# Outputs of experts 0 to 6 turned by VectorE in squares of 32 and scattered as quarter rows

## The chip, the cores and the metric

The kernel runs on one core of one Trainium2 chip. The metric is the time of one execution on the device in microseconds (us); the median of three runs stands for the kernel. A profile is one further execution, recorded by the hardware profiler. Its span goes from the first to the last instruction.

The engines named below are TensorE (PE in the profile; PEld are its loads of the stationary operand), VectorE (DVE), ScalarE (ACT), GpSimd (POOL) and SyncE (SP), which only issues transfers. All data of this kernel are 32-bit floats.

## The reference

Attention with a threshold comes first, and its output is the input of a layer of experts to which tokens are assigned by a hash:

```python
batch, n_heads, seq, head_dim = (8, 8, 576, 64)        # attention
N, D, E, F = (4608, 512, 8, 1024)                      # experts

scores = scale * np.matmul(q, k.transpose(0, 1, 3, 2))
thresh = np.max(scores, axis=-1, keepdims=True) - tau
scores = np.where(scores >= thresh, scores, -1000000000.0)
attn = softmax(scores); x = attn @ v                   # x: (B*S, H*D)

expert_idx = token_ids * np.int64(2654435761) % np.int64(E)
for e in range(E):
    mask = expert_idx == e
    h = np.maximum(x[mask] @ w1[e], 0.0)
    out[mask] = h @ w2[e]
```

So 4608 tokens of 512 numbers each go through one of 8 experts, some 576 to each: two matrix products (512 to 1024, then 1024 to 512) with a ReLU between them. Each result row goes to its token's place in `out`.

## The kernel before, in words

**Stages.** Until about 480 us the kernel computes attention and writes x to a scratch tensor in memory (`x_scratch`); beside it, it sorts the tokens by expert (`route`, `scatters`). Then come the experts, one after the other. Only this second stage, and a few preparations at the end of the first (lines 812 to 820), are touched by the change.

**Tokens in slots.** Each expert has 608 slots, of which `caps` are used: 576 for the first five in the order of processing, 600 for the last three. Tokens without a slot go through a loop at the end. A slot is a pair (s, c): column 32 s + c of the expert's matrices, with s up to 18 and c up to 31. The table `stok` holds the token number of each slot; its 32 rows c stand four times, in each of the four groups of 32 partitions. `gidx`, copied from it, holds for 128 consecutive columns, one per partition, the token number to which the result goes.

**Features on partitions.** Both layers work on transposed data: x of an expert is `xT` (512 features as 4 blocks of 128 partitions, and a column for each slot), the hidden layer `h_0` has 8 such blocks, and the result is `oT` with 4. The stationary operand of a matmul is a block of a weight matrix (`w1_sb`, `w2_sb`), the moving operand 288 or 300 columns of `xT` or `h_0`.

**Seven products.** `seven` (line 908) computes a layer by Strassen's scheme in the form with seven products of half matrices. VectorE forms the sums of half matrices: `sums_w1`, `sums_w2` (four tensor_tensor instructions of 1024 elements a partition each, one of them in place in `w2_sb`), `sums_x` and `sums_h` (half as wide). In layer 1 the scheme runs twice (g = 0 and 1), with 8 matmul records for each product; in layer 2 once, with 16 for each. The order of the products is fixed: p1 (copied out of PSUM by ScalarE), c11, u2, u3, c21, one product that gives both u4 and c22, and c12. Six instructions of VectorE add a product from PSUM to a partial sum, and one product is read by two adds. A product lies in one of four PSUM tiles of two banks (`bank2`), which are used in turn; the document calls such a tile a bank.

**Order of the work.** The stage is written under a manual schedule: each engine takes its instructions in the order of the code. Side work is hung between the products by a callback with the number of the step (0 after c11, 1 after u2, 2 after u3, 3 after c21, 4 after c22, 5 after c12):

- in group 0 of layer 1 (`side1`) one sum of w2 at each step, and at step 0 the output of the expert before, `put_out(e - 1, (0, 1), (2, 3), (4,))`
- in group 1 of layer 1 the sums of the first half of h, and from step 3 of group 0 on the squares of the next x (`turns`)
- in layer 2 (`side2`) at step 0 what is left of the turns, then `fetch`, which has GpSimd gather the rows of x for the expert after the next (five indirect transfers), and from step 1 on the sums of the next w1 and x, two at a step.

The next x is turned without TensorE: VectorE transposes the gathered rows in squares of 32 (line 1025), and 16 transfers of SyncE move them into `xT` (line 1033).

**How an output leaves (before).** `put_out` turns `oT` back to rows. For each 128 columns TensorE does 8 transposes into a PSUM tile (line 989), 40 for an expert, in three PSUM tiles from the same ring of four. ScalarE copies each 128 rows to an output tile `o_sb`, of which there are three (line 1001), and GpSimd issues an indirect transfer that scatters 128 rows of 2 KB to their places in `out` (line 1005). The last expert's output leaves in smaller pieces during and after its own layer 2.

Of the kernel before, what the change touches and what calls it, by code (L numbers as in the profile page):

```python
# [9 lines left out]
FP32 = mybir.dt.float32  # L10
BF16 = mybir.dt.bfloat16
FP16 = mybir.dt.float16
I32 = mybir.dt.int32
# [7 lines left out]
def kernel(  # L21
# [81 lines left out]
    stok_odd = consts.tile([P, E, NB], I32, name="stok_odd")  # L103


    gidx = consts.tile([P, E, KT], I32, name="gidx")
    gidx_0 = consts.tile([P, KT, HP], I32, name="gidx_0")
    sidx = [consts.tile([P, KT], I32, name=f"sidx_{i}") for i in range(2)]
    gidx_x = consts.tile([P, E, KT], I32, name="gidx_x")
# [35 lines left out]
    with tc.tile_pool(name="a_q", bufs=1) as a_q, \  # L145
# [450 lines left out]
        def constants():  # L596

            nc.gpsimd.iota(iota_i[:], pattern=[[1, NOV]], base=0, channel_multiplier=0)
            nc.gpsimd.tensor_copy(iota_f[:], iota_i[:])
            make_upper_triangular(nc, u128[:], val=1.0, diag=False)  # L600
            nc.gpsimd.memset(ones128[:], 1.0)
            nc.gpsimd.memset(none[:], BIG)
            nc.gpsimd.memset(gidx[:], BIG)
            nc.gpsimd.memset(gidx_x[:], BIG)
            for t in sidx:
                nc.gpsimd.memset(t[:], BIG)
            nc.gpsimd.iota(tok[:], pattern=[[1, NTC]], base=0, channel_multiplier=NTC)
            for table in slot_dram:
                nc.sync.dma_start(out=table.rearrange("(p c) o -> p (c o)", p=P), in_=none[:])
# [83 lines left out]
        with tc.manual_schedule():  # L693
# [118 lines left out]
            nc.vector.tensor_tensor(out=stok[:], in0=stok[:], in1=stok_odd[:], op=ALU.min)  # L812
            for h in range(4):
                rows, n = slice(32 * h, 32 * h + 32), (NB - h + 3) // 4
                nc.vector.tensor_copy(gidx[rows, :, 0:n], stok[rows, :, h::4])
                nc.vector.tensor_copy(gidx[rows, E - 1, KT - 1:KT],
                                      stok[rows, E - 1, NB - 4 + h:NB - 3 + h])
            for g in range(4):
                rows, n = slice(32 * g, 32 * g + 32), min(KT, NB - KT * g)
                nc.vector.tensor_copy(gidx_x[rows, 1:, 0:n], stok[rows, 1:, KT * g:KT * g + n])  # L820
            for _ in pieces:
                pass
            for kt in range(KT):
                fetch_0(kt, HP - 1)
            fill(FO * 2 * (CO - 1) - 18)
# [3 lines left out]
    with tc.tile_pool(name="m_x", bufs=1) as m_x, \  # L829
         tc.tile_pool(name="m_o", bufs=3) as m_o, \  # L830
         tc.tile_pool(name="m_s", bufs=1) as m_s:

        F2, C2, FH, D2, NG = F // 2, CO // 2, FO // 2, DIN // 2, FO // 4
        xT_bufs = [xT_0, m_x.tile([P, CO, CAP], FP32, name="xT_1")]
        xq = m_x.tile([P, DIN // 32, 32 * KT], FP32, name="xq")
        oT = m_x.tile([P, CO, CAP], FP32, name="oT")
        o_end = m_x.tile([P, DIN], FP32, name="o_end")
        mark = m_x.tile([P, 1], FP32, name="mark")
        w1_s = m_s.tile([P, 3, C2, F2], FP32, name="w1_s")
# [27 lines left out]
        def w1_blocks(w):  # L867
            return [w[:, C2 * j:C2 * j + C2, F2 * i:F2 * i + F2] for i in range(2) for j in range(2)]

        def w2_blocks(w):  # L870
            return [w[:, FH * j:FH * j + FH, D2 * i:D2 * i + D2] for i in range(2) for j in range(2)]

        def x_blocks(e):
            x, half = xT_bufs[e % 2], caps[e] // 2
# [16 lines left out]
        def sums_w2(e):  # L891
            s1 = None
            if e == E - 1:
                spare = w_pool.tile([P, CO, F], FP32, name="w1_sb")
                s1 = w_tiles["s1"] = spare[:, :, 0:D2]
            return left(*w2_blocks(w_tiles[e, 2]), triple(w2_s, 0, FH), s1)

        def sums_x(e):
            return right(*x_blocks(e), triple(x_s, 0, C2, caps[e] // 2))
# [8 lines left out]
        def seven(a, a_s, b, b_s, m0, outs, relu, after):  # L908

            (a11, a12, s1, a22), (s2, s3, s4) = a, a_s  # L910
            (b11, t1, b21, b22), (t2, t3, t4) = b, b_s
            c11, c12, c21, c22 = outs
            n_k, width = a11.shape[1], b11.shape[2]
            p1, u2, u3, u4 = (t[:, :, 0:width] for t in halves)

            def product(x, y):
                ps = bank2()
                for i in range(2):
                    c0 = m0 + P * i
                    for c in range(n_k):  # L920
                        nc.tensor.matmul(ps[:, i, 0:width], lhsT=x[:, c, c0:c0 + P], rhs=y[:, c],  # L921
                                         start=c == 0, stop=c == n_k - 1)
                return ps[:, :, 0:width]

            def out(c, ps, u, step):
                add(c, ps, u)()
                if relu:
                    nc.scalar.activation(c, c, AF.Relu)  # L928
                after(step)

            nc.scalar.copy(p1, product(a11, b11))  # L931
            out(c11, product(a12, b21), p1, 0)
            add(u2, product(s2, t2), p1)()
            after(1)
            add(u3, product(s3, t3), u2)()
            after(2)
            out(c21, product(a22, t4), u3, 3)
            k5 = product(s1, t1)
            add(u4, k5, u2)()
            out(c22, k5, u3, 4)  # L940
            out(c12, product(s4, b22), u4, 5)
# [10 lines left out]
        def layer2(e, side):  # L952

            w, half = w_tiles[e, 2], half2(e)
            outs = [oT[:, C2 * i:C2 * i + C2, half * k:half * k + half]
                    for i in range(2) for k in range(2)]
            a = w2_blocks(w)
            if e == E - 1:
                a[2] = w_tiles["s1"]
            seven(a, triple(w2_s, 0, FH), h_blocks(0, FH, half),  # L960
                  triple(h_s, 0, FH, half), 0, outs, False, side)

        def last_tile(middle):

            w, o_sb, idx = w_tiles[E - 1, 2], o_end, gidx[:, E - 1, KT - 1:KT]
            rows = CAP - 2 * CHL
            for c0, c1 in ((0, DIN - P), (DIN - P, DIN)):
                ps = bank2()
                for fo in range(FO):
                    nc.tensor.matmul(ps[0:rows, 0, 0:c1 - c0], lhsT=h_0[:, fo, 2 * CHL:CAP],  # L970
                                     rhs=w[:, fo, c0:c1], start=fo == 0, stop=fo == FO - 1)
                    if (c0, fo) == (0, FH - 1):
                        middle()
                nc.scalar.copy(o_sb[0:rows, c0:c1], ps[0:rows, 0, 0:c1 - c0])
            put_rows(o_sb[0:rows], idx[0:rows])

        def put_out(e, *groups):

            def rows_of(kt):
                return t_rows(e, kt) if e < E - 1 or kt < KT - 2 else 2 * CHL - FIRST[kt]  # L980

            trs = [bank2() for _ in groups]
            for tr, kts in zip(trs, groups):
                for i, kt in enumerate(kts):
                    rows = rows_of(kt)
                    for co in range(CO):
                        for r in range(2):
                            half, c0 = slice(64 * r, 64 * r + 64), D2 * i + 64 * co
                            nc.tensor.transpose(tr[0:rows, r, c0:c0 + 64],
                                                oT[half, co, FIRST[kt]:FIRST[kt] + rows],  # L990
                                                ident[half, half])
            for tr, kts in zip(trs, groups):
                for i, kt in enumerate(kts):
                    rows = rows_of(kt)
                    o_sb = m_o.tile([P, DIN], FP32, name="o_sb")
                    dst = o_sb[0:rows].rearrange("p (c r q) -> p r c q", c=CO, r=2)
                    src = tr[0:rows, :, D2 * i:D2 * i + D2].rearrange("p r (c q) -> p r c q", c=CO)
                    if e == E - 1 and kt % 2:
                        nc.vector.tensor_copy(dst, src)
                    else:  # L1000
                        nc.scalar.copy(dst, src)  # L1001
                    put_rows(o_sb[0:rows], gidx[0:rows, e, kt:kt + 1])

        def put_rows(o_sb, idx, ordered=False):
            inst = nc.gpsimd.indirect_dma_start(  # L1005
                out=out[:, :], out_offset=bass.IndirectOffsetOnAxis(ap=idx, axis=0),
                in_=o_sb, in_offset=None, bounds_check=N - 1, oob_is_err=False)
            inst = getattr(inst, "ins", inst)
            if ordered:
                return  # L1010
            tc.declare_no_dep(inst, group="rows", reason="every token has one slot: distinct rows")
            tc.add_to_no_dep_group("rows", inst)
# [35 lines left out]
        with tc.manual_schedule():  # L1048
            for e in range(E):
# [3 lines left out]
                if e > 0:  # L1053
                    w2_work, h_work = sums_w2(e), sums_h(e, 0, 2)

                    def side1(g, step):
                        if g == 0:
                            run(w2_work)
                            if step == 0:
                                put_out(e - 1, (0, 1), (2, 3), (4,))  # L1060
                        else:
                            run(h_work)
                        if step > 2:
                            run(turns, 1 if g == 0 else 2)

                    layer1(e, side1)
                    run(sums_h(e, 2, FH), 4)
# [4 lines left out]
                def side2(step):  # L1072
# [3 lines left out]
                            fetch(e + 2)  # L1076
                    else:
                        run(x_work, 2)
                    if not more and step == 4:
                        put_out(e, (0,))  # L1080

# [84 lines left out]
```

## Time and profile before

| what | value |
|---|---|
| median of the runs | 944.61 us (943.98 to 944.72) |
| profiled execution, its own time | 938.01 us |
| its span | 936.4 us, clock of TensorE 0.997 |
| TensorE busy | 919.9 us (98%) |
| VectorE busy | 731.2 us (78%) |
| ScalarE busy | 476.4 us (51%) |
| GpSimd busy | 308.6 us (33%) |
| transposes of L989, TensorE | 312 in 11.5 us |
| evictions of L1001, ScalarE | 37 of 584 ns |
| scatters of L1005, GpSimd | 39 of 1192 ns |
| squares of L1025, VectorE | 35 of 691 ns |

The profiled execution is 6.6 us (0.7%) shorter than the median of the runs; the profile is used for durations and for where the time lies. The busy time of TensorE is a union of pipelined, modelled records, so the starts of its matmuls tell more than its busy share. In the table of groups a line says: source line, engine, operation, output and inputs, shapes and count, then busy time in us, the mean of one instruction in ns, the idle time of the engine just before them and what ended it. Line numbers are those of the kernel before; in the changed kernel they are up to 34 higher.

### The profile page before, as it was taken

How to read it: one execution, taken by the hardware profiler on the slowest of the kernel's cores; microseconds unless marked ns; L12 is line 12 of the kernel's file. 1: busy time of each engine (PE TensorE's matmuls, PEld its weight loads, DVE VectorE, ACT ScalarE, POOL GpSimd, SP SyncE). 2: the span in 40 equal slices, each digit the busy share in tenths (PEclk: the TensorE clock that was granted, in tenths of full speed). 3: DMA queues.
4: the chain of work that ended last, by engine and by line, in shares of the span. 5: the costliest groups of instructions: out<-in, count | busy, mean ns of one | idle time of the engine just before them, and what ended most of it. 6: DMA issues, size and time to landing. Idle time of an engine off the chain costs nothing.

```text
span 936.4 us, 21124 instructions
## 1 busy us (share of the span) xinstructions
PE 919.9 (98%) x7775; PEld 643.1 (69%) x7775; DVE 731.2 (78%) x1643; ACT 476.4 (51%) x776; POOL 308.6 (33%) x424
## 2 busy tenths in 40 slices
PE   8999999999999999999999999999999999999996
PEld 4666666666666666666577777777777777777785
DVE  8999999999999999999457665756667566675541
ACT  6888888888988988988511120202112031120310
POOL 4233332336676643556135210403013030100202
PEclk9999999999999999999999999999999999999998
DMA  7355464464456776751016545254443544311101
GB/s 176 92 144 128 105 145 116 111 150 113 93 128 190 180 167 161 199 135 47 18 25 206 168 98 186 83 158 156 103 180 99 154 153 141 137 51 29 53 1 53
DMA packets 113351, 113.12 MB, mean 121 GB/s; under 512 B 31018, under 2 KB 87866, under 8 KB 113248
## 3 DMA queue, kind: packets, MB, share of 16 engines
q1 hardware_dynamic: 105168, 92.64, 37.5%
q0 software_dynamic: 7648, 18.91, 6.9%
q8 instruction: 63, 1.03, 0.5%
q14 instruction: 40, 0.33, 0.1%
q10 hardware_dynamic: 432, 0.21, 0.1%
HBM read 81.99 MB, written 21.47 MB: 110 GB/s over the span
## 4 chain that ended last, share of the span: by engine, by line
PE 61%; issue 29%; DVE 3%; ACT 2%; POOL 2%; DMA 2%; POOLq 0%; SPq 0%; DVEq 0%; ACTq 0%
PE av L314 18%; PE sc L236 15%; PE bank L921 12%; PE tr L283 11%; PE sc L645 3%; PE av L283 1%; POOL out_dram L1005 1%; DMA out_dram<-o_sb,gidx 1%; ACT w L261 1%; DVE xq L1025 1%; DVE h L854 1%; POOL xg L120 1%; DVE ns L247 0%; PE xT_ps L663 0%; PE sc L663 0%
## 5 line engine op out<-in xcount | busy, mean ns | idle before, releaser
L261 ACT ACTIVATE w<-ns,nmx 128x576 f32<-128x576 f32 x288 | 220.3, 776 | 34.3 <-DVE ns L247 33.9
L272 DVE SCALAR_TENSOR_TENSOR w<-ns,thr,w 128x576 f32<-128x576 f32 x288 | 226.4, 818 | 0.0
L247 DVE TENSOR_SCALAR_CACHE_REDUCE ns<-sc 128x576 f32<-128x576 f32 x288 | 205.3, 744 | 3.5 <-PE sc L236 2.7
L236 PE MATMUL sc<-k_sb,q 64*128 64x288 f32 (+1 forms) x1280 | 178.6, 423 | 0.9 <-DVE ns L247 0.7
L283 PEld LDWEIGHTS tr<-ident,w 64*128 64x128 f32 x2624 | 106.3, 138 | 88.0 <-ACT wT_b L304 25.7
L254 POOL TENSOR_SCALAR thr<-nmx,drop 128x2 f32<-128x2 f32 (+1 forms) x160 | 105.0, 656 | 180.9 <-DVE ns L247 168.9
L283 PE MATMUL tr<-ident,w 64*128 64x64 f32 x2624 | 138.7, 230 | 2.4 <-ACT wT_a L304 2.0
L1005 POOL DMA_INDIRECT out_dram<-o_sb,gidx x39 | 46.5, 1192 | 284.4 <-ACT o_sb L1001 269.5
L931 ACT COPY p<-bank 128x576 f32<-128x576 f32 (+2 forms) x22 | 14.1, 642 | 195.3 <-PE bank L921 195.0
L236 PEld LDWEIGHTS sc<-k_sb,q 64*128 64x128 f32 (+1 forms) x1280 | 92.0, 177 | 24.0 <-DVE ns L247 10.7
L314 PE MATMUL av<-wT_a,v 128*64 128x320 f32 (+1 forms) x704 | 100.4, 418 | 0.4 <-DVE xm L353 0.3
L928 ACT ACTIVATE h<-h 128x576 f32<-128x576 f32 (+1 forms) x56 | 38.8, 692 | 117.5 <-DVE h L854 117.3
L921 PE MATMUL bank<-h,w_sb 128*128 128x288 f32 (+2 forms) x384 | 94.9, 404 | 0.8 <-DVE h L668 0.8
L304 ACT COPY wT_a<-tr 128x512 f32<-128x512 f32 (+1 forms) x128 | 81.7, 638 | 20.0 <-PE tr L283 19.5
L921 PE MATMUL bank<-xT,w_sb 128*128 128x288 f32 (+1 forms) x336 | 87.5, 410 | 0.0
L921 PEld LDWEIGHTS bank<-h,w_sb 128*128 128x128 f32 x384 | 72.9, 190 | 20.5 <-DVE h L668 1.3
L304 ACT COPY wT_b<-tr 128x512 f32<-128x512 f32 (+1 forms) x128 | 81.2, 634 | 4.9 <-PE tr L283 2.6
L314 PE MATMUL av<-wT_b,v 128*64 128x256 f32 x640 | 83.2, 389 | 0.0
L921 PEld LDWEIGHTS bank<-xT,w_sb 128*128 128x128 f32 x336 | 63.8, 190 | 19.1
L314 PEld LDWEIGHTS av<-wT_a,v 128*64 128x64 f32 x704 | 43.7, 136 | 29.2 <-DVE xm L353 0.8
L921 PE MATMUL bank<-h_s,w_s 128*128 128x288 f32 (+2 forms) x256 | 62.7, 404 | 0.0
L120 POOL DMA_INDIRECT xg<-x_scratch,gidx_x x35 | 36.4, 1041 | 68.7 <-DVE xq L1025 52.5
(163 smaller groups left out, 1121.4 us busy)
## 6 DMA issues: line engine op xcount, KB each, us to landing
w_sb<-in_moe_w_dram SPq DMA_DIRECT2D x16, 2048.0 KB
q<-in_q_dram SPq DMA_DIRECT2D x62, 288.0 KB
v<-in_v_dram SPq DMA_DIRECT2D x32, 256.0 KB
x_scratch<-xm SPq DMA_DIRECT2D x32, 256.0 KB
xT<-xq SPq DMA_DIRECT2D x84, 80.0 KB
k_sb<-in_k_dram SPq DMA_DIRECT2D x31, 144.0 KB
k_sb<-in_k_dram SPq DMA_DIRECT2D x32, 112.0 KB
x_scratch<-xg SPq DMA_DIRECT2D x9, 256.0 KB
```

What stands on the lines that cost most here:

```text
L120: nc.gpsimd.indirect_dma_start(out=dst, out_offset=None, in_=src, in_offset=bass.IndirectOffsetOnAxis(ap=idx, axis=0), bounds_check=src.sh ...
L236: nc.tensor.matmul(sc[out_rows, i, 0:S2], lhsT=q_sb[rows, h, q0:q1], rhs=k_sb[rows, h], start=True, stop=True)
L247: nc.vector.tensor_scalar(out=ns[:].rearrange("p (i s) -> p i s", i=2), in0=sc[:, :, 0:S2], scalar1=-1.0, scalar2=None, op0=ALU.mult, op1= ...
L254: nc.gpsimd.tensor_scalar(out=thr[:, 0:j + 1], in0=stats[n][0][:, 0:j + 1], scalar1=drop[:], scalar2=None, op0=ALU.add)
L261: nc.scalar.activation(w, nss[n, j][:], AF.Exp, bias=stats[n][0][:, j:j + 1], scale=-1.0)
L272: nc.vector.scalar_tensor_tensor(out=w, in0=nss.pop((n, j))[:], scalar=stats[n][1][:, j:j + 1], in1=w, op0=ALU.is_le, op1=ALU.mult, accum_ ...
L283: nc.tensor.transpose(dst[:, r, 64 * c:64 * c + 64], src[rows, c0:c0 + P], ident[rows, rows])
L304: nc.scalar.copy(dst, tr[:, :, 0:64 * n_c].rearrange("p r (c q) -> p r c q", c=n_c))
L314: nc.tensor.matmul(av[64 * j:64 * j + 64, g, c0:c1], lhsT=v_sb[:, c, 64 * j:64 * j + 64], rhs=wT[g][:, i, c0:c1], start=(c == 0), stop=stop)
L921: nc.tensor.matmul(ps[:, i, 0:width], lhsT=x[:, c, c0:c0 + P], rhs=y[:, c], start=c == 0, stop=c == n_k - 1)
L928: nc.scalar.activation(c, c, AF.Relu)
L1005: inst = nc.gpsimd.indirect_dma_start(out=out[:, :], out_offset=bass.IndirectOffsetOnAxis(ap=idx, axis=0), in_=o_sb, in_offset=None, bound ...
```

## The change

**Which features a block holds.** Until now block i of layer 2's output held the features 128 i to 128 i + 127. For experts 0 to 6 it now holds every fourth: partition p of block i has feature 4 p + i. For this the columns of w2 are taken with a step: `dealt` views a row of w2 as (m, b), m being 128 numbers and b the block, and `w2_blocks` and the matmuls of layer 2 read with it. The stationary operand from `w2_sb` has a step of four floats, the one from the sums `w2_s`, which are stored as pairs of blocks, a step of two. The sums read two neighbouring floats out of every four. Expert 7 is as before.

**The turning.** `put_squares(e, i)` replaces `put_out` for experts 0 to 6. One VectorE instruction transposes all squares of 32 of one half of an expert's slots, 9 in the first half and 9 or 10 in the second. After it, partition 32 g + q of `o_q` holds for each square s the features 128 g to 128 g + 127 of the token in slot (s, q): a quarter of an output row, 512 bytes, written by the instruction with a step of four floats. TensorE, PSUM and ScalarE take no part.

**The scatter.** `out` is seen as 18432 rows of 128 numbers, and each square goes out with one indirect transfer of 128 such rows (64 KB). The row number is four times the token number plus the partition group: a table `qidx` of 152 numbers a partition, made once by one VectorE instruction from `stok` and a constant `quart`. An expert has 18 or 19 of these transfers, 128 in all, where it had 5.

**When.** The first half (`put_squares(e, 0)`) is issued in the expert's own layer 2 after step 3, the second half (`put_squares(e - 1, 1)`) at step 0 of group 0 in layer 1 of the next expert, where `put_out` stood.

**Beside it.** `oT` has 8 columns more, which GpSimd sets to zero once, since squares reach to slot 608. `gidx` is kept for the last expert alone, and its copies are smaller.

```diff
-    gidx = consts.tile([P, E, KT], I32, name="gidx")
+    gidx = consts.tile([P, KT], I32, name="gidx")
+    quart = consts.tile([P, 1], I32, name="quart")
+    qidx = consts.tile([P, E, NB], I32, name="qidx")
...
+            for g in range(4):
+                nc.gpsimd.memset(quart[32 * g:32 * g + 32, :], g)
...
-                nc.vector.tensor_copy(gidx[rows, :, 0:n], stok[rows, :, h::4])
+                nc.vector.tensor_copy(gidx[rows, 0:n], stok[rows, E - 1, h::4])
...
+            nc.vector.scalar_tensor_tensor(
+                out=qidx[:], in0=stok[:], scalar=4.0,
+                in1=quart[:, :, None].to_broadcast([P, E, NB]), op0=ALU.mult, op1=ALU.add)
...
+        NH = LOW // 64
+        out_q = out.rearrange("n (g m) -> (n g) m", g=4)
-        oT = m_x.tile([P, CO, CAP], FP32, name="oT")
+        oT = m_x.tile([P, CO, SL], FP32, name="oT")
+        o_q = [m_x.tile([P, n, 32, CO], FP32, name=f"o_q{i}") for i, n in enumerate((NH, NB - NH))]
+        nc.gpsimd.memset(oT[:, :, CAP:SL], 0.0)
...
+        def dealt(x, n):
+            return x.rearrange("p f (m b) -> p f m b", b=n)
+
+        def w2_blocks(e, w):
+            if e == E - 1:
+                return [w[:, FH * j:FH * j + FH, D2 * i:D2 * i + D2]
+                        for i in range(2) for j in range(2)]
+            return [dealt(w[:, FH * j:FH * j + FH], CO)[:, :, :, C2 * i:C2 * i + C2]
+                    for i in range(2) for j in range(2)]
+
+        def w2_sums(e):
+            t = triple(w2_s, 0, FH)
+            return t if e == E - 1 else [dealt(x, C2) for x in t]
...
-                        nc.tensor.matmul(ps[:, i, 0:width], lhsT=x[:, c, c0:c0 + P], rhs=y[:, c],
+                        lhsT = (x[:, c, :, i] if dealt_out else
+                                x[:, c, c0:c0 + P])
+                        nc.tensor.matmul(ps[:, i, 0:width], lhsT=lhsT, rhs=y[:, c],
...
+        def put_squares(e, i):
+
+            s0, s1 = ((0, NH), (NH, -(-caps[e] // 32)))[i]
+            nc.vector.transpose(
+                out=o_q[i][:, 0:s1 - s0].rearrange("p n a c -> p c n a"),
+                in_=oT[:, :, 32 * s0:32 * s1].rearrange("p c (n q) -> p c n q", q=32))
+            for s in range(s0, s1):
+                put_rows(o_q[i][:, s - s0].rearrange("p a c -> p (a c)"), qidx[:, e, s:s + 1],
+                         rows=out_q)
...
                             if step == 0:
-                                put_out(e - 1, (0, 1), (2, 3), (4,))
+                                put_squares(e - 1, 1)
...
+                    if more and step == 3:
+                        put_squares(e, 0)
```

## The prediction

> **What bounds the kernel now.** I read the page first: TensorE is busy 98% of the span, and from about 496 us on (the expert stage, everything the change touches but small preparations) its two rows in the 40 slices show nines with a clock of 9. So there a microsecond can be gained only by giving TensorE less to do or by closing a hole in its stream. Then I read TensorE's timeline around one change of expert, which shows what the output's turning costs (columns: start, length, engine, line, operation, count, and in brackets an idle time with its releaser):
>
> ```profile
> 636.29 4.04 PE L921 MATMUL bank<-xT,w_sb 128*128 128x288 f32 x16
> 640.26 1.44 PE L989 MATMUL bank<-ident,oT 64*128 64x64 f32 x40
> 641.63 4.15 PE L921 MATMUL bank<-x_s,w_s 128*128 128x288 f32 x16
> 646.15 2.21 PE L921 MATMUL bank<-x_s,w_sb 128*128 128x288 f32 x8 [0.37 <-ACT o_sb L1001]
> 648.19 2.10 PE L921 MATMUL bank<-xT,w_sb 128*128 128x288 f32 x8
> 650.13 2.10 PE L921 MATMUL bank<-xT,w_s 128*128 128x288 f32 x8
> 652.07 4.04 PE L921 MATMUL bank<-xT,w_sb 128*128 128x288 f32 x16
> ```
>
> Undisturbed, 8 matmuls take 650.13 - 648.19 = 1.94 us, a pitch of 242.5 ns. The 40 matmuls from 636.29 to 648.19 should take 9.70 us and take 11.90: 2.20 us are lost, to 40 transposes of the last expert's output (about 1.56) and to a wait for a PSUM bank that ScalarE has still to empty into an output tile (about 0.64, with the refill). Everywhere else between 496 and 916 us the matmuls follow each other at their pitch; the bound is TensorE, and these two holes are its only loss.
>
> Next, VectorE in the same stretch, because the change gives it the turning:
>
> ```profile
> 696.96 0.76 DVE L854 TENSOR_TENSOR h<-bank,p 128x576 f32<-128x576 f32 x1 [3.19 <-PE bank L921]
> 697.64 1.22 DVE L851 TENSOR_TENSOR w_s<-w_sb 128x1024 f32<-128x1024 f32 x1
> 700.40 0.76 DVE L854 TENSOR_TENSOR u<-bank,p 128x576 f32<-128x576 f32 x1 [1.54 <-PE bank L921]
> 701.07 1.22 DVE L854 TENSOR_TENSOR w_sb<-w_sb 128x1024 f32<-128x1024 f32 x1
> 702.34 0.76 DVE L854 TENSOR_TENSOR u<-bank,u 128x576 f32<-128x576 f32 x1
> ```
>
> That is no bound, but is close to one: after the first sum of w2 there are 1.54 us idle, then instruction follows instruction.
>
> **Part 1, removed: 40 transposes and 5 evictions for each of experts 0 to 6.** The same sum (start of the third group after the transposes, minus start of the group before them, minus 40 pitches) for the seven: 1.57 at 527 us, 2.56 at 583, 2.20 at 640, 2.21 at 697, and with the 252.5 ns pitch of 600-wide experts 2.09 at 753, 2.10 at 812, 2.11 at 871. Sum 14.84 us, all on TensorE's path: 7 x 1.56 = 10.95 of transposes, 3.89 of bank waits. The bank wait goes too, since the change takes no PSUM bank for the turning. ScalarE's 35 copies go (585 ns each); it is busy 10 to 20% there, worth nothing. Expert 7 keeps its way.
>
> **Part 2, added on VectorE: two square transposes for each expert** (1152 elements a partition; 1280 in the second of experts 5 and 6). The square row, 128x512 at 691 ns, lies on the line of the tensor_tensor rows (757 at 576, 1358 at 1152: 1.04 ns an element), so 1152 cost 1.36 us. New is that they write every fourth float, 16 bytes apart. No row writes so; two rows read so:
>
> ```profile
> L483 DVE TENSOR_REDUCE rank_f<-incl 128x36 f32<-128x288 f32 x1 | 0.7, 695 | 0.0
> L536 DVE TENSOR_REDUCE ovf<-keep 128x32 f32<-128x256 f32 x1 | 0.4, 420 | 0.0
> L815 DVE COPY gidx<-stok 32x40 int32<-32x40 int32 x3 | 0.5, 183 | 0.1
> L820 DVE COPY gidx_x<-stok 32x35 int32<-32x35 int32 x3 | 0.5, 179 | 0.0
> ```
>
> L483 reads at 144 bytes' distance, L536 side by side. With 420 - 256 x 1.04 = 154 ns fixed, L483 takes (695 - 154)/288 = 1.88 ns an element: 0.84 more. L815 reads at 16 bytes' distance and pays nothing (5 elements more than L820, 4 ns more). The square is thus 1.36 us by the row with its own distance, 2.32 by the other. I take 1.36 and keep 2.32.
>
> Does VectorE keep up? The tight place is group 0 of layer 1, which has the second square, the four sums of w2 and three squares of x. Count from the group's first matmul, product k ending at 1.94k. VectorE starts on product 2 at about 4.18 (696.96 - 692.81 = 4.15). Until product 6's bank is free it has six adds (c11, u2, u3, c21, u4, c22) at 0.68 (starts 696.96 and 697.64), 4.08; four sums at about 1.24, 4.96; one x square, 0.63; and the new square. The queue ends at 4.18 + 4.08 + 4.96 + 0.63 + 1.36 = 15.21 us, or 16.17 with 2.32. That bank is wanted (four in turn) by product 3 of group 1, at 9 x 1.94 = 17.46. So TensorE never waits, with 2.25 or 1.29 us to spare, and the later adds and the h sums catch up in group 1, whose VectorE work is 7 x 0.68 + 4 x 0.69 + 2 x 0.63 = 8.8 us of 13.6. Cost nothing; uncovered, the square would cost its excess over 3.6 us, seven times.
>
> The first square of each expert stands in layer 2 before the add u4, where products last 3.9 us; the x sums behind it end at 692.0 and are wanted by product 3 at 692.81 + 3.88 = 696.7. Nothing, but for expert 0: there the x sums wait for the moved x until 522.2, the third one ends at 525.75, the square before it makes that 527.1 (or 528.1), and product 3 starts at 523.52 + 3.88 = 527.4. Between 0 and 0.7 us, once.
>
> **Part 3, moved: layer 2's weights are read with a step.** The four sums of w2 read two floats of four: same element count, so 1.24 us; if each element paid L483's price they would take 1024 x 1.88 + 154 = 2.08. The weight loads read every fourth float of `w_sb` (four of seven products) or every second of `w_s`: 7 x 4 x 16 = 448 loads of the first kind, 336 of the second.
>
> ```profile
> L921 PEld LDWEIGHTS bank<-h,w_sb 128*128 128x128 f32 x384 | 72.9, 190 | 20.5 <-DVE h L668 1.3
> L314 PEld LDWEIGHTS av<-wT_a,v 128*64 128x64 f32 x704 | 43.7, 136 | 29.2 <-DVE xm L353 0.8
> ```
>
> 64 columns more cost 54 ns: 0.84 ns a column and some 82 fixed, so a load occupies the load path 108 ns. Instruction by instruction the trace agrees: at 641.627 a load starts into an empty engine, and the next follows 108 ns later with the first matmul. Each load starts with the matmul before it and has that matmul's 242 ns: it is hidden up to 242/128 = 1.89 ns a column. The Trainium skill, page "Advanced Engine Details and Errata", section "SBUF Cachelines", speaks against the change here: SBUF's lines have 16 bytes, two hits on a line are needed to hide the memory's latency, and a reader that meets a new line at every access pays. It gives no price. By that rule the loads with step four pay on every column, those with step two do not (nor do the sums). With L483 as the price: if a line takes 1.88 ns a load is 241 ns, just hidden; if 0.84 adds to 0.84, 1.68 x 128 = 215, hidden; if 1.88 adds to 0.84, 348 ns, 106 too long, 448 x 106 = 47.5 us. By L815, the row with the same distance, nothing. I take nothing and keep 47.5.
>
> **Part 4, added on GpSimd and its queue: 128 scatters of 64 KB for 35 of 256 KB.** An issue is 1.19 us (L1005, mean) and 0.30 to the next. An expert now has 18 or 19 x 1.5 = 27 to 28.5 us and 5 gathers x 1.3 = 6.6: 34 of the 54.3 us that an expert takes. Behind the second nine scatters (from about 644.7 in the stretch above) wait the gathers of x: they would run from 658 to 666 instead of 651 to 666.6, and their rows are first used by the x squares of the next expert, at 706. Each scatter also waits, in the built program, for the transfer eight before it: landing takes 2.6 to 3.5 us (trace of L1005), eight issues 10.4. ScalarE no longer feeds the scatters. Bytes are the same; if every extra row of 512 bytes took a full packet of queue 0 (6.9% x 16 x 936.4 us / 7648 = 135 ns), 12,000 rows would be 101 us for each of 16 engines over 390, where the page shows 1 to 6 tenths busy. SP's queue gets nothing new; x's move has 10 us (end 675.1, sums at 685.9). Nothing.
>
> **Part 5, preparations.** The clearing of the tail of `oT` lies on GpSimd before the last gathers, inside an idle time of 17.2 us. The row numbers cost one instruction of 152 elements on VectorE, 0.31 us as L812, less 0.15 saved on smaller copies. The h copies behind it have some 0.3 us: 0 to 0.2.
>
> **Sum.** 936.4 us of span (938.01 with what lies around it) - 14.84 + 0.3 (expert 0 and the preparations) = 921.9 of span. The median of the runs shown is 944.61, 6.6 over the profiled execution; the same difference gives **930.1**.
>
> **Rivals.** (a) VectorE becomes the bound in group 0: for this the row L483 speaks, against it L815. With sums of 2.08 and squares of 2.32 product 6's bank comes free at 19.53, 2.07 us late, times 7 is 14.5: 944.3, no gain. With one of the two only it is up to 1.1 late: 930 to 938. (b) Slower: the weight loads of layer 2 at a step of four outlast a matmul. It decides from 14.5 us/448 = 32 ns, that is from 274 ns or 2.14 ns a column, 2.5 times today's; at 348 ns the time is 930.1 + 47.5 = 977.6. The rule speaks for it, L815 and the spare factor of 2.25 against. (c) GpSimd's queue delays x, so that the gain is partly lost: it needs over 40 us of lateness, or landings over 10.4 us. (d) The holes don't close, because something else fills them: in the trace nothing but the transposes and the bank wait stands there.
>
> **Numbers.** As forecast, 929 to 933: 0.66. Gain partly eaten (a in part, c), 933 to 942.7: 0.13. Within 0.2% (1.9 us, about what a measurement of this kernel can tell from none): 0.05, nearly all (a). Slower, (b) and what is like it: 0.16. Range 929 to 943, which leaves out the slower case and a little below.
>
> **What would show it.** No L989 transposes before 916 us, and matmul groups at their pitch from 496 to 902 (changes of expert 54.3 us apart, from 56.5). Two squares an expert of 1.4 to 2.3 us. Weight loads of layer 2 of 190 to 325 ns with matmuls still at 242; more, and matmuls at the load's pitch, means (b). A bracket of PE waiting for VectorE in group 1 means (a). Scatters in runs of nine, 1.3 to 1.5 us apart.

## The result and the profile after

| | before | after |
|---|---|---|
| median of the runs, first chip | 944.30 us (943.92 to 944.72) | 933.88 us (930.1 to 935.01) |
| profiled execution, its own time | 938.01 us | 933.93 us |
| its span | 936.4 us | 932.2 us |
| first matmul of the experts, in the span | 496.3 us | 502.9 us |
| from there to the end | 440.1 us | 429.3 us |

After divided by before is 0.9883 [0.9854, 0.9911]: 10.4 us faster, where 14.5 were forecast. On a second chip, in the experiments below, the same kernel is 14.2 us faster. Two things are to be explained: where the gain comes from, and what took some 4 us of it on the first chip.

In the profile shown the experts begin 6.6 us later than before, though the change does nothing there that could take 6.6 us. It is as much as the runs of before stood above their own profile; that both have one cause is likely and not shown. That profile of before, at 938.01 us, lies outside the first chip's runs of before (943.92 to 944.72) and inside those of the second (937.1 to 938.99), so no profile shows the kernel before as it runs at 944.3. The span is therefore compared from the first expert matmul on: 440.1 to 429.3, a gain of 10.8.

First TensorE's timeline of the changed kernel, at the same change of expert as before (columns as there; `L945` was `L921`):

```profile
643.67 4.04 PE L945 MATMUL bank<-xT,w_sb 128*128 128x288 f32 x16
647.55 4.04 PE L945 MATMUL bank<-x_s,w_s 128*128 128x288 f32 x16
651.43 2.10 PE L945 MATMUL bank<-x_s,w_sb 128*128 128x288 f32 x8
653.37 2.10 PE L945 MATMUL bank<-xT,w_sb 128*128 128x288 f32 x8
655.31 2.10 PE L945 MATMUL bank<-xT,w_s 128*128 128x288 f32 x8
657.25 4.04 PE L945 MATMUL bank<-xT,w_sb 128*128 128x288 f32 x16
```

The transposes are gone, and so is the wait in brackets. From 643.67 to 653.37 the 40 matmuls take 9.70 us, exactly 40 pitches of 242.5 ns, where they took 11.90.

Then VectorE's timeline in the same stretch, with the new square (`L1031`) in it:

```profile
647.82 0.76 DVE L865 TENSOR_TENSOR h<-bank,p 128x576 f32<-128x576 f32 x1 [3.19 <-issue]
648.50 1.22 DVE L862 TENSOR_TENSOR w_s<-w_sb 128x1024 f32<-128x1024 f32 x1
649.63 2.26 DVE L1031 STREAM_TRANSPOSE o_q<-oT 128x1152 f32<-128x1152 f32 x1
651.73 0.74 DVE L865 TENSOR_TENSOR u<-bank,p 128x576 f32<-128x576 f32 x1
...
657.73 0.72 DVE L865 TENSOR_TENSOR u<-bank,u 128x576 f32<-128x576 f32 x1
658.38 0.75 DVE L865 TENSOR_TENSOR h<-bank,u 128x576 f32<-128x576 f32 x1
```

VectorE makes seven adds of products in a group, not six; c12 is the seventh. The last line shown is c22, the add that frees the bank of product 6. It ends at 659.13, 15.46 us after the group's first matmul; the bank is wanted at 17.46. There are 2.0 us to spare.

The groups that carry the new costs (line, engine, operation, shapes and count, then busy us, mean ns, idle before and its releasers):

```profile
L1031 DVE STREAM_TRANSPOSE o_q<-oT 128x1152 f32<-128x1152 f32 x12 | 27.2, 2269 | 0.0
L862 DVE TENSOR_TENSOR w_s<-w_sb 128x1024 f32<-128x1024 f32 x28 | 34.0, 1215 | 0.0
L945 PEld LDWEIGHTS bank<-h,w_sb 128*128 128x128 f32 x384 | 92.5, 294 | 4.2 <-issue 1.9
L945 PEld LDWEIGHTS bank<-h_s,w_s 128*128 128x128 f32 x256 | 50.0, 195 | 13.3 <-DVE h_s L862 2.3
L1039 POOL DMA_INDIRECT out_dram<-o_q,qidx x128 | 141.0, 1102 | 194.8 <-DVE o_q L1031 133.8
```

A square costs 2.27 us. The sums of w2 cost what they did. The weight loads of layer 2 from `w_sb` rose from a mean of 190 to 294 ns; taken by themselves nearly all the loads with a step of four take 307 to 309 (the 294 mixes in expert 7, which reads side by side). Those from `w_s`, with a step of two, rose from 190 to a mean of 195.

Last, the place of the loss. In the profile on the first chip every expert from the third on takes what the sum gave it, 54.32 or 56.56 us, but the second in the order of processing, which the table further down calls expert 1, takes 59.06. Its TensorE timeline, with two lines of VectorE's:

```profile
558.05 6.95 PE L945 MATMUL bank<-h,w_sb 128*128 128x288 f32 x28
565.96 0.40 PE L945 MATMUL bank<-h,w_sb 128*128 128x288 f32 x1 [0.95 <-issue]
566.86 1.11 PE L945 MATMUL bank<-h,w_sb 128*128 128x288 f32 x3 [0.50 <-issue]
566.90 0.76 DVE L865 TENSOR_TENSOR h<-bank,u 128x576 f32<-128x576 f32 x1 [6.06 <-remote]
567.81 1.13 PE L945 MATMUL bank<-h_s,w_s 128*128 128x288 f32 x4
570.79 0.76 DVE L862 TENSOR_TENSOR h_s<-h,h_s 128x576 f32<-128x576 f32 x1
570.81 4.40 PE L945 MATMUL bank<-h_s,w_s 128*128 128x288 f32 x17 [1.86 <-DVE h_s L862]
```

The 32 matmuls from 558.05 should be followed by the next product at 558.05 + 7.76 = 565.81; it begins at 567.81, after two stops of TensorE for which the profile knows no reason ("issue"). Four matmuls later TensorE waits for `h_s`, which VectorE computes late, because its add of 566.90 stood 6.06 us for TensorE's signal that product 7 of layer 1 was done ("remote" is a release that the profile puts down to no instruction; the semaphore, a counter by which engines signal each other, is the one that TensorE's products raise). The last matmul of that product had started before 558.05, so the signal came more than 8.8 us after that start. The product goes on at 570.81, where an unbroken stream would have had it at 565.81 + 4 x 0.2425 = 566.78: 4.0 us lost in all.

### The profile page after: what moved, and what is told of

Read it like the earlier page. It is cut to its first block, busy times and chain, and to the rows that moved or that the text cites. A ratio compares the mean times of both kernels' runs of the same rounds, so it can differ in the third digit from the quotient of the medians.

```text
span 932.2 us, 20728 instructions
## 1 busy us (share of the span) xinstructions
PE 911.4 (98%) x7495; PEld 662.9 (71%) x7495; DVE 759.5 (81%) x1658; ACT 458.3 (49%) x741; POOL 408.1 (44%) x522
## 3 DMA queue, kind: packets, MB, share of 16 engines
q0 software_dynamic: 9104, 18.91, 7.2%
## 4 chain that ended last, share of the span: by engine, by line
PE 62%; issue 21%; POOL 8%; DVE 3%; DMA 2%; ACT 2%; another core or an unknown queue 1%; SPq 1%; POOLq 0%; DVEq 0%; ACTq 0%
PE av L316 18%; PE sc L238 15%; PE bank L945 13%; PE tr L285 11%; POOL out_dram L1039 6%; PE sc L649 3%; PE av L285 1%; POOL xg L122 1%; DMA xT<-xq 1%; ACT w L263 1%; DMA xg<-x_scratch,gidx_x 1%; DMA k_sb<-in_k_dram 1%; ACT wT_b L306 1%; SPq L1067 0%
## 5 line engine op out<-in xcount | busy, mean ns | idle before, releaser
L263 ACT ACTIVATE w<-ns,nmx 128x576 f32<-128x576 f32 x288 | 220.4, 777 | 28.5 <-DVE ns L249 28.2
L1039 POOL DMA_INDIRECT out_dram<-o_q,qidx x128 | 141.0, 1102 | 194.8 <-DVE o_q L1031 133.8
L945 PE MATMUL bank<-h,w_sb 128*128 128x288 f32 (+2 forms) x384 | 95.6, 405 | 2.3 <-issue 1.5
L945 PEld LDWEIGHTS bank<-h,w_sb 128*128 128x128 f32 x384 | 92.5, 294 | 4.2 <-issue 1.9
L945 PE MATMUL bank<-xT,w_sb 128*128 128x288 f32 (+1 forms) x336 | 87.5, 410 | 0.0
L945 PEld LDWEIGHTS bank<-xT,w_sb 128*128 128x128 f32 x336 | 63.8, 190 | 19.0
L945 PE MATMUL bank<-h_s,w_s 128*128 128x288 f32 (+2 forms) x256 | 63.0, 404 | 1.9 <-DVE h_s L862 1.9
L945 PEld LDWEIGHTS bank<-h_s,w_s 128*128 128x128 f32 x256 | 50.0, 195 | 13.3 <-DVE h_s L862 2.3
```

Source lines behind the costliest of these rows:

```text
L263: nc.scalar.activation(w, nss[n, j][:], AF.Exp, bias=stats[n][0][:, j:j + 1], scale=-1.0)
L945: nc.tensor.matmul(ps[:, i, 0:width], lhsT=lhsT, rhs=y[:, c], start=c == 0, stop=c == n_k - 1)
L1039: inst = nc.gpsimd.indirect_dma_start(out=rows[:, :], out_offset=bass.IndirectOffsetOnAxis(ap=idx, axis=0), in_=o_sb, in_offset=None, boun ...
```

## The experiments

All four kernels ran on one chip, called the second here, where the kernel before has 937.94 us (937.46 to 938.99, 19 runs). That the first runs came from another chip is not shown here by more than the 6.4 us between 944.30 and 937.94. In the expectations of the second and third, theory A says that the hole in expert 1 belongs to the change (18 scatters in one run on GpSimd's queue, the gathers behind them, and their transfers together with the move of x), theory B that it belongs to a chip or to single executions, as the longer attention stage does.

### The kernel before, again

No edit.

> The kernel before, unchanged, for a second profile. In its first profile the expert stage began at 496.3 us and took 440.1; in the profile after it began at 502.9 and took 429.3. If the attention stage simply varies between executions, this profile begins the expert stage anywhere from 496 to 503 and again takes 440 us there, and its time is 938 or 944 accordingly. If the change made the attention stage longer (its tables, the clearing of oT, other addresses), the expert stage begins at 496 again and the runs at 944 have their 6 us elsewhere.

Measured: 937.83 us (937.1 to 938.32), ratio 0.9996 [0.9987, 1.0006]. Two sets of runs of one kernel on one chip agree within 0.1%, so the 6.5 us between this and the 944.30 of the first chip are no scatter of single runs. The experts begin at 496.2 us of the profile and last 440.3, as in the first profile of before.

### The changed kernel, again

No edit.

> The changed kernel, unchanged, for a second profile. Theory A: the hole of 4.2 us that TensorE has in expert 1 (564 to 571 us) belongs to the change: behind 18 scatters in a row GpSimd issues the five gathers of x at 558 to 564, just as SyncE moves the x before it, and the products' completion comes up to 9 us late. Then it stands in this profile too, and the time is 933 to 935. Theory B: it is a disturbance of single executions. Then it is away or elsewhere here, and runs lie at 930 as often as at 934.

Measured: 923.75 us (922.05 to 923.8), ratio 0.9845 [0.9828, 0.9861], a gain of 14.2 us. The experts begin at 495.7 us. TensorE's timeline at the place of the hole, with VectorE's line for the same add:

```profile
548.30 2.10 PE L945 MATMUL bank<-xT,w_s 128*128 128x288 f32 x8
549.78 1.42 DVE L865 TENSOR_TENSOR h<-bank,u 128x576 f32<-128x576 f32 x2
550.24 7.92 PE L945 MATMUL bank<-h,w_sb 128*128 128x288 f32 x32
558.00 2.35 PE L945 MATMUL bank<-h_s,w_s 128*128 128x288 f32 x9
```

No hole: 7.76 us from 550.24 to 558.00, 32 pitches, and the add of product 7 is done at 551.20 without a wait. And yet GpSimd's order is the same here, by its timeline on this chip:

```profile
548.49 0.98 POOL L1039 DMA_INDIRECT out_dram<-o_q,qidx  x1 [0.30 <-issue]
549.77 1.05 POOL L122 DMA_INDIRECT xg<-x_scratch,gidx_x  x1 [0.30 <-issue]
...
555.47 0.99 POOL L122 DMA_INDIRECT xg<-x_scratch,gidx_x  x1 [0.30 <-issue]
```

The last scatter is followed by the five gathers, under the move of x (SyncE's 16 transfers, 549.27 to 560.03), as on the first chip (gathers 558.23 to 564.50, move 557.07 to 568.65). So that order and that meeting of transfers are not enough to make the hole. In its plain form theory A falls.

The profile on the first chip also lost time earlier, where the work is that of the kernel before. These are the sums from 200 to 440 us, in the attention stage, for the changed kernel on the first chip and then on the second. After the window and its length come busy us and number of instructions of TensorE, its loads, VectorE, ScalarE and GpSimd, then the granted clock, the busy share of the DMA engines and GB/s:

```profile
200.00:440.00 240.00, 236.31 (x2932) 148.33 (x2928) 233.48 (x643) 206.97 (x337) 137.64 (x184) 1.00 0.58 144
200.00:440.00 240.00, 240.00 (x3010) 151.72 (x3012) 238.52 (x661) 212.32 (x347) 142.52 (x189) 1.00 0.58 144
```

The clock and the transfers are the same, and yet TensorE gets through 78 matmuls fewer and stands still several times, at most for 1.69 us:

```profile
433.21 0.52 PE L285 MATMUL tr<-ident,w 64*128 64x64 f32 x10 [1.69 <-ACT wT_b L306]
```

Its rows of ScalarE (`L263`) run 0.6 us behind those of after_again at 212 us and 7.0 at 434. In each of the other five profiles, four kernels in all, TensorE is busy 240.00 of these 240 us, with 3010 to 3016 matmuls. TensorE's signals, too, are odd all through that one profile: in the expert stage 48 of the 154 matmuls of `seven` that raise its semaphore have no raise on record within 0.1 us of their end (it came late or was not recorded), and in the other five profiles every one has. So the disturbance is there before the change has its first square to scatter, which speaks for theory B. What it is, the traces don't tell.

The times between the first matmuls of two experts, in us, put the gain where it is (the first row counts from the first matmul of the experts, the last to the end of the span):

| | before_again | after, first chip | after_again | late_scatter | step_only |
|---|---|---|---|---|---|
| expert 0 | 27.26 | 27.39 | 27.39 | 27.39 | 27.39 |
| expert 1 | 55.89 | 59.06 | 54.32 | 54.32 | 55.88 |
| expert 2 | 56.82 | 54.32 | 54.32 | 54.32 | 56.85 |
| expert 3 | 56.52 | 54.32 | 54.32 | 54.32 | 56.54 |
| expert 4 | 56.53 | 54.32 | 54.32 | 54.32 | 56.53 |
| expert 5 | 58.66 | 56.56 | 56.56 | 56.56 | 58.66 |
| expert 6 | 58.67 | 56.56 | 56.56 | 56.56 | 58.65 |
| expert 7 to the end | 69.9 | 66.8 | 67.0 | 67.0 | 69.9 |

From before_again to after_again experts 1 to 6 gain 1.57, 2.50, 2.20, 2.21, 2.10 and 2.11. Expert 7 gains 2.9; 0.8 of it lies behind the start of the last scatter (7.5 us to the end of the span against 6.7), where the change does nothing.

### The second half's scatters behind the gathers

The squares stay where they are; the nine or ten scatters of the second half are issued in layer 2, after `fetch` has issued the gathers. Nothing is left out.

```diff
-        def put_squares(e, i):
+        def put_squares(e, i, send=True):
...
-                                put_squares(e - 1, 1)
+                                put_squares(e - 1, 1, not more)
...
+                        if e > 0 and more:
+                            send_squares(e - 1, 1)
```

> The changed kernel with the nine or ten scatters of an expert's second half (not their square) issued in layer 2 of the next expert, behind its gathers, instead of at step 0 of layer 1; the last pair of experts as it was. Theory A: the gathers are issued as the x squares end, three of them before the move of x, the hole in expert 1 goes and the time falls by some 4 us to 930. Theory B: no difference to the changed kernel beyond its own scatter.

Measured: 922.83 us (922.62 to 923.91), ratio 0.9838 [0.9821, 0.9854], the same as after_again within the intervals. GpSimd's timeline shows that the edit did what it says, a gather and then the scatters of the half before:

```profile
551.05 1.00 POOL L122 DMA_INDIRECT xg<-x_scratch,gidx_x  x1 [0.30 <-DVE u L865]
552.35 1.02 POOL L1044 DMA_INDIRECT out_dram<-o_q,qidx  x1 [0.30 <-issue]
```

Experts 0 to 6 take the same time to 0.01 us, and expert 7 to 0.02: where the scatters stand on GpSimd's queue is worth nothing here, as part 4 of the prediction had it. Since the changed kernel shows no hole on this chip either, the run can't tell what the other order would have done on the first chip.

### The kernel before with the step in layer 2's weights alone

`dealt`, `w2_blocks`, `w2_sums` and the stepped operand of the change are put into the kernel before; the transposes, the copies and the five scatters stay. The numbers of a row of `out` of experts 0 to 6 then stand in another order; the work is the same in kind and size.

```diff
-            return left(*w2_blocks(w_tiles[e, 2]), triple(w2_s, 0, FH), s1)
+            return left(*w2_blocks(e, w_tiles[e, 2]), w2_sums(e), s1)
...
-                        nc.tensor.matmul(ps[:, i, 0:width], lhsT=x[:, c, c0:c0 + P], rhs=y[:, c],
+                        lhsT = (x[:, c, :, i] if dealt_out else
+                                x[:, c, c0:c0 + P])
+                        nc.tensor.matmul(ps[:, i, 0:width], lhsT=lhsT, rhs=y[:, c],
```

> The kernel before with part 3 of the change alone: layer 2 of experts 0 to 6 reads w2 with a step of four and its sums with a step of two; the outputs still leave by TensorE, ScalarE and 35 scatters, so that the features of these experts' rows stand in another order than in the reference. Theory: the weight loads take 308 ns as in the profile after, of which 226 occupy the load path, and stay hidden under matmuls of 242 ns: same time as before within 0.2%, the holes at each change of expert unchanged at 2.1 to 2.2 us. Rival: part of what the change did not bring (it brought 10.4 us of 14.5) is lost here: 2 to 4 us slower than before, with matmuls of layer 2 over 242 ns apart.

Measured: 938.03 us (937.33 to 938.96), ratio 0.9999 [0.9989, 1.0009]. The loads of this kernel, in its table of groups:

```profile
L934 PEld LDWEIGHTS bank<-h,w_sb 128*128 128x128 f32 x384 | 92.4, 294 | 2.3 <-DVE h L668 1.3
L934 PEld LDWEIGHTS bank<-h_s,w_sb 128*128 128x128 f32 x128 | 31.0, 294 | 0.5
L934 PEld LDWEIGHTS bank<-h,w_s 128*128 128x128 f32 x128 | 24.9, 195 | 5.4
```

and the same groups of the kernel before on that chip:

```profile
L921 PEld LDWEIGHTS bank<-h,w_sb 128*128 128x128 f32 x384 | 72.9, 190 | 20.5 <-DVE h L668 1.3
L921 PEld LDWEIGHTS bank<-h_s,w_sb 128*128 128x128 f32 x128 | 24.3, 190 | 6.4
L921 PEld LDWEIGHTS bank<-h,w_s 128*128 128x128 f32 x128 | 24.2, 190 | 6.4
```

448 loads are longer by 118 ns each, 52.9 us of load time, and the kernel takes no longer. In the idle time before the loads one sees what paid: 20.5 us of the first group shrank to 2.3, 6.4 of the second to 0.5. This also means that nothing of the gain comes from the new order of features; it comes from taking the turning off TensorE.

One load has nothing in front of it to hide under, the first of expert 0's layer 2, where TensorE has waited for VectorE. Its weight load and the next in before_again, then in step_only:

```profile
496.21 0.19 PEld L921 LDWEIGHTS bank<-h,w_sb 128*128 128x128 f32 x1 [1.30 <-DVE h L668]
496.32 0.19 PEld L921 LDWEIGHTS bank<-h,w_sb 128*128 128x128 f32 x1
496.49 0.31 PEld L934 LDWEIGHTS bank<-h,w_sb 128*128 128x128 f32 x1 [1.30 <-DVE h L668]
496.70 0.33 PEld L934 LDWEIGHTS bank<-h,w_sb 128*128 128x128 f32 x1
```

The second load follows after 0.11 us with the plain read and after 0.21 with the step. The second matmul starts 0.12 us later with it, and this is the 0.13 us by which expert 0 is longer in every profile with the step.

### What was not tried

Squares written side by side, squares doubled, scatters doubled, and expert 7's weight loads with the step were not run. So the cause of the square's price, the exact room of VectorE and of GpSimd's queue, and what a load of this length does under the narrower matmuls of expert 7 rest on the traces above, not on an edit.

## Why the prediction was right, and where it was wrong

**What bounds the kernel.** Right. With 14.8 us of transposes and waits gone TensorE is still busy 98 to 99% of the span, its stream without a hole on the second chip. What the profiles show of gain are these holes, but for 0.8 us at the program's end.

**Part 1, removed.** Right to a few hundredths. The seven losses were put at 1.57, 2.56, 2.20, 2.21, 2.09, 2.10 and 2.11; measured are 1.57, 2.50, 2.20, 2.21, 2.10, 2.11, and 2.1 of the last (the rest of its 2.9 lies at the program's end). The intervals of 54.3 us were foretold and are there. Rival (d), that something else fills the holes, falls.

**Part 2, the squares.** The time was right, the price wrong. 1.36 us was taken from `L815`, 2.32 was kept from `L483`; measured is 2.27 us, or (2269 - 154)/1152 = 1.84 ns an element, close to the 1.88 of `L483`. (The larger squares, 1280 elements in 2490 ns, give 1.73 by the difference of the two sizes.) The choice "nearest row" went by the distance of 16 bytes alone, but that row reads a few numbers with a step, while the square writes 1152 so. That the step is what costs is argued: the squares of x (`L1059`), which write 32 numbers side by side, stayed at 695 ns for 512 elements, but a square of the output with a plain write was not run. Nothing is lost by it: product 6's bank comes free at 15.46 us, where the sum with 2.32 gave 16.17, and it is wanted at 17.46. The sum was too high because it used durations; from start to start a sum of w2 occupies VectorE for 1.13 us and not 1.24, and the square 2.10 and not 2.27. Rival (a) needed slow sums and slow squares together; only the squares were slow.

Expert 0's 0 to 0.7 us came out at both ends. In the profile on the first chip product 3 of expert 1 waits 0.36 us for an x sum, and the stream is some 0.6 late behind it; in after_again, where the moved x arrives earlier (3.98 us of wait against 5.42), nothing is lost. This wait is 3.8 to 5.5 us in the six profiles, and on the second chip 3.79 in before_again and 5.25 in step_only, so it goes with the execution and not with the chip.

**Part 3, the weight loads.** The time was right, the price wrong again in the same way, and here the right time was luck. "Nothing" was taken by `L815`; the loads with a step of four take 308 ns. By the prediction's reckoning that is 308 - 82 = 226 of the load path, and by the two loads shown above 213, 1.7 to 1.8 ns a column against 0.84. Of the ends that the prediction kept from `L483`, 215, 241 and 348, the first is nearest. The Trainium skill, page "Advanced Engine Details and Errata", section "SBUF Cachelines", spoke for a price, and its rule held in sign and place: a new 16-byte line at every column costs (118 ns a load), two numbers of each line nearly nothing (5 to 8 ns a load, and the sums of w2 at 1.22 us as before). It says nothing about the size, and the size decided. 213 to 226 ns lie under the matmul's 242.5, by 16 to 30 ns. Rival (b) falls, shown by the step alone in the kernel before; but the cover was 7 to 12%, not the factor of 2.25 that the prediction spoke of.

**Part 4, the scatters.** Right. 1.10 us each and 0.30 to the next, 1.40 from start to start where 1.49 was reckoned; GpSimd's order is worth nothing. The gathers of expert 3's stretch were expected some 22 us after its first matmul; in after_again, one expert earlier, the first starts at 599.79, 22.4 after 577.40. Rival (c), a delay of x that eats the gain, is not seen on the second chip. One detail was wrong: they don't come in runs of nine. The first half is still being issued when the second half's square is done, so 18 go out in a row. The bound on the extra packets was far too high, too: queue 0 has 9104 packets after 7648, 1456 more, not 12,000, and 7.2% of the engines' time after 6.9%.

**Part 5** is too small to be seen: the row numbers' instruction takes 333 ns where 0.31 us was given. The 0.13 us of expert 0 are the stepped load's, which part 3 had at nothing.

**The sum.** 14.5 us were forecast, 14.2 measured on the second chip and 10.4 on the first. The first chip's 933.88 lies just above the band of 929 to 933 that had the chance of 0.66, in the one that was kept for (a) and (c); neither of the two is what the profile shows there. The term that the sum lacks is the hole in expert 1, 4.0 us; with some 0.6 for the late x sum of the expert change it is nearly the whole of the 4.74 us between 59.06 and 54.32. Among the four runs on the first chip one lies at 930.1 and three from 933.83 to 935.01, so that it may be a matter of one execution and not of the chip; one profile can't tell. The run at 930.1 stands 6.4 us above the second chip's median, just as the kernel before does; that it equals the forecast to the digit is chance. Two slips in the sums change nothing: 7 x 1.56 is 10.92, not 10.95, and rival (a) would come to 930.1 + 14.5 = 944.6, not 944.3.

**What stays open** is its cause. Shown is that TensorE's signal for product 7 came more than 8.8 us after the last matmul's start, that TensorE itself paused twice for 1.45 us in all by "issue", and that neither the order on GpSimd's queue nor the meeting of gathers with the move of x is sufficient for it. Three more adds of layer 1 stand for such late signals in that profile, up to 3.1 us each, and cost TensorE nothing; in the other five profiles there is no such wait. The same execution was already behind at 440 us, in work that the change leaves alone. So the hole is more likely part of a disturbed execution than of the change, but this is argued: the kernel before lost 6.4 us on the first chip and the changed one 10.1, and whether the change makes a disturbance dearer can't be told without a profile of before that has it.

## What to carry to other kernels

When the engine at the bound is without holes, moving side work to one with a measured slack returns what it took, here on the second chip to 0.3 us of 14.5. When a profile of the changed kernel lies off, look first at a stretch that the change leaves alone: here 200 to 440 us had lost time as well, which no reading of the changed stage would have shown. A stepped operand is not free because a small copy with the same step was: take its price from a row of the same engine and size, or keep the high end, and compare it with what covers it. Estimated from these numbers, a load that holds the path for 213 to 226 ns is covered only by matmuls of more than 253 to 268 columns (242.5 ns/288 = 0.842 a column), so the same edit under narrower tiles would set TensorE's pace; no run here has narrow tiles and the step together.

## What the runs showed of the hardware

- A weight load of 128 columns of 32-bit floats takes 190 ns side by side, 195 to 198 with a step of 8 bytes and 307 to 309 with a step of 16. Under matmuls 242.5 ns apart none of them is felt; where nothing covers it, the last one costs 0.12 us.
- A transposing write of VectorE with a step of 16 bytes takes 1.84 ns an element; the 32-square with whole stretches of 32 takes 695 ns for 512, (695 - 154)/512 = 1.06 ns. That the step is the cause was not tried.
- A signal of TensorE's completion can come more than 8.8 us after its last matmul started, in an execution that is behind in other stages too, while the same kernel in a second profile shows no such wait. The waiting engine has "remote" as its releaser.
- One kernel, before, runs at 944.3 us in one set of runs and at 937.9 in another, put down to two chips, each set within 0.2%; the differences between two kernels are to be taken within one set.
